# Second gate of a three-layer kernel: half of the rectifier of token chunks 0 and 1 moved to ScalarE, and a new order of its instructions

## The chip, the cores and the metric

The kernel runs on one core of a Trainium2 chip. The metric is the device time of one execution in microseconds (us). TensorE (PE in the profile, PEld for its weight loads) multiplies, VectorE (DVE), ScalarE (ACT) and GpSimd (POOL) do the elementwise work, and the queue of SyncE (SP) issues nearly all transfers. Each engine works through its own instructions strictly in order.

## What is computed

Attention in the Nystroem form gives 2304 rows of 512 values. Two gated layers follow; the change lies in the second one and in the order of everything around it.

```python
def _moe_ref(x, w_in, w_out):
    h = x @ w_in
    return ((h * np.cos(h)) @ w_out)

def _moe2_ref(x, w_in, w_out, alpha):      # x: 2304x512, w_in: 512x2048, w_out: 2048x512
    h = x @ w_in
    g = np.maximum(h, 0.0) + alpha * np.minimum(h, 0.0)
    return (g @ w_out)
```

`alpha` has one value for each of the 2048 columns of `h`. In the kernel `h` lies transposed, so that `alpha` is one value for each partition.

## The kernel before

Every matmul operand is split into a rounded high part and the remainder, and a product is the sum of three matmuls (high by high, high by low, low by high). A split costs a copy to the rounded type on ScalarE and a subtraction (`sub`, line 414) on VectorE or GpSimd.

The first gate runs in 128 ticks, t0 to t127 in the order table (lines 1063 to 1088). The second gate takes the 2304 tokens in four chunks of 512 and one of 256. Each chunk has eight ticks; a tick makes 256 of the 2048 hidden columns, as 128 and 128. Ticks b0 to b7 are chunk 0, b8 to b15 chunk 1, and so on to b39. This text calls them by these names.

In chunks 0 and 1 a tick is `btick`. Its `h` comes from seven Strassen products of six matmuls each (`strassen`, line 1425 in the trace), written into two banks of PSUM that appear as `h` and `x`. Four short copies take partial sums out of these banks (`keep`; line 409 when on ScalarE, 411 when on VectorE): two of them go to the buffer `sa`, two to `sb`, and there is one of each buffer. Some products write again the quarter of a bank that a copy has just emptied, so they wait for that copy. Two additions on VectorE (`cross`, line 1448) then put the tick's 128x1024 result together in the buffer `H`: the first frees bank `x` and `sb`, the second bank `h` and `sa`.

Then each half of the tick (128x512) goes through the rectifier: on VectorE, line 1721 makes alpha\*min(h,0) and line 1724 adds max(h,0). Line 1726 rounds the result on ScalarE, line 414 makes the remainder, and twelve matmuls of 512 columns (line 1738) multiply it by `w_out` and add into four banks `acc`.

Chunks 2 and 3 use `mtick` with `narrow` (products in line 1469, copies through line 409 or 411, additions in line 1481) and a Strassen form of the second product too (line 1620). Their rectifier has a first half on ScalarE: line 1555 makes max(h,0), line 1557 makes max(-h,0) in place, and line 1559 on VectorE multiplies the latter by -alpha (`minus`) and adds. Chunk 4 has a direct product (line 1524) and its rectifier on VectorE alone.

Weights of the second gate are made once, spilled to DRAM (`wf2d`) and loaded again for each chunk from chunk 1 on, into buffers that are used again as soon as the last product has read them (line 1267 issues these loads; `y_load`, `load_wo2` and `t_make` load the rest).

The order is written out: `ORDER` is a table of some 4,200 names, and `Plan.go` emits the operations in that order, each on the engine that its suffix names. So the table decides what stands before what on every engine, and which of two engines does a copy or a subtraction. Buffers and waits follow from the data.

Of the kernel before, what the change touches and what calls it, by code (L numbers as in the profile page):

```python
# [142 lines left out]
t120:7/V y0:29 y0:18 t118:9 t119:9 t123:1 t122:2 o1:2 t121:7/V t122:3 t118:10 t118:8 t120:9 t119:8 t119:10 t120:8 y0:9
t122:4 t123:2 y0:34 y0:15/V y0:10/V t122:5 s64:10 t123:3 t123:4 t123:5 y0:39 t122:6 t124:1 y0:35/V o9:2 y0:30 t122:7
t123:6 t123:7 o1:3 t120:10 t121:10 t121:9 t125:1 t122:9 t123:9 t120:11 t121:8 t121:11 y0:19 t124:2 t124:3 t124:4 t124:5
t127:1 t122:8 t125:2 y0:27 t125:3 y0:28/V t125:4 y0:20 s65:3 o9:3 t125:5 y0:40/V t127:2 t127:3 t124:6 t127:4 t122:10
t123:10 t126:1 t122:11 t123:8 t123:11 t124:7/V t125:6 t126:2 o10:1 o11:1 s65:1 s64:25 c62:5 o0:1 t124:8 t127:5 t127:6
t125:7 t127:7/V t126:3 t126:4 t126:5 t126:6 t126:7/V o10:2 b0:1 b0:2 b0:4 t124:9 b0:3/V b0:5 b0:6/V b0:7 b0:8 b0:9 b0:10
b0:13 b0:11 b0:12 b0:14 o11:2 o11:3/V o10:3 t125:8 b1:1 o4:1 s65:4 s64:7 t124:10 b1:2 b1:4 b1:5 o0:2 b1:3 o4:2 s65:8
t126:8 o8:1 b0:15 o0:3/V o6:1 t125:9 t124:11 t126:9 s65:5 s65:11 s65:9/V s65:6/V b1:6/V s65:14/V s65:18/V s65:22/V  # L150
s65:15 s65:16/V s65:12/V s65:26/V t125:11 t126:11 t127:11 t125:10 t126:10 b1:7 b1:8 t127:10 b1:9 b1:10 b2:1 t127:8 o8:2
b0:16 o6:2 s65:10 o4:3/V s65:27 e127:5/V b0:22 b2:2 s65:28/V b2:4 s65:17 s66:3 b1:13 s65:23 s65:24 s65:19 b2:3 b1:11/V
b1:12 s65:20 b2:5 t127:9 s65:13 s65:25 b2:7 b2:6 b2:8 b2:9 b2:10 b3:1 b3:2 o8:3/V b0:23 b0:17 e127:2 s65:7 b1:14 b2:13
e127:1 e127:4 b0:24 b0:25 b0:20 b1:15 b1:22 b1:16 b2:11 b0:21 b0:18 b3:4 s66:4 s66:2 b1:23 b1:17/G o6:3 b2:12 b3:5
b3:3/V b3:7 s66:11 b3:6 b1:24 e127:6 s65:29 s66:8 s66:1 b0:19 e127:3 s66:12/V b2:22 b3:8 s66:5 b3:9 s66:6 s66:13 b1:25/G
s66:9/V s66:14/V s66:15 s66:16/V b2:23 b2:14 s66:18/V s66:22 o3:1 s66:17 s66:10 s65:21 o2:1 b0:26 b1:18 s66:26/V o3:2
s66:27 s66:23 s66:24 b2:15 s66:28/V s66:7 o12:1 b3:10 b4:1 b3:13 b3:11/V b2:24 s66:19 s66:20 s67:2 s66:25 b0:27 b0:28
b4:2 b0:29 b2:16 b4:3/V b4:4 b4:5 o2:2 b2:25/G b1:19 b1:27 b1:21 b1:20 b1:28 s67:1 b3:12 b2:17/G s66:29 b4:7 b4:6 b1:26
s67:3 b4:8/V b1:29 b4:9 b4:10 b5:1 b5:2 b5:4 s67:4 b4:13 o2:3/V b2:19 b2:27 b5:5 b3:14 b3:15 o3:3/V s67:8 b3:16 b3:17/G
o14:1 s66:21 b4:11/V b5:3/V b2:18 b2:20 b2:21 b2:28 s67:5 b4:12 b3:22 b2:26 b3:18 b5:6/V b3:20 s67:11 s67:12/V b3:23  # L160
b4:22 b3:24 s67:6/V b4:23 s67:9/V s67:14/V b3:25 b4:14 b5:7 s67:15 b5:8 b5:9 s67:18 s67:22 o13:1 o13:2 o13:3/V s67:26/V
b2:29 b3:21 b3:19 s67:23 o12:2 b5:10 b6:1 b6:2 b3:29 b4:15 o12:3/V s67:24/V b5:11 b4:16 s67:16/V o14:2 b5:12 b5:13 o14:3
# [10 lines left out]
b10:3/V b10:6/V b7:19 b9:15 b10:7 b10:9 b10:8 b7:27 b10:10 b10:11 b8:24 b8:25 b11:1 b11:2 b11:4 x7:2 b7:37 s69:2 b9:16
b10:12 b9:17 b9:22 b9:23 b10:13 b10:14 b11:5 b9:24 b9:25 b7:29 b8:21 b8:19 b8:27 b7:30 b11:3/V x7:3/V b8:18 b11:6/V
b10:15 x7:4/V b11:7 b8:20 b11:8/V b11:9 b11:10 x7:11 b10:16 s69:7 s69:4 x7:5 x7:6 b8:28 b9:20 b8:29 b9:19 x7:9 x7:7
b11:11 b7:28 s69:1 x7:12/V b10:22 b10:23 b11:12 x7:8 s69:3 x6:2 b10:17 b9:21 b9:29 x6:1 b8:26 s69:5 b10:24 b10:25 b11:13
x6:3 x6:4 x7:10 b9:18 b9:26 b11:22 b11:23 s69:6 x6:11 x6:12 b7:31 b11:14 b11:15 x5:1 b11:16 b11:24 b12:1 b12:2 b12:3/V
x6:5 x5:2 b11:25 b11:17 b12:4 b12:5 b9:28 b12:7 b12:6 b12:8 b12:9 b10:20 b12:10 b13:1 b13:2 b13:4 s70:1 b12:11 x6:7
b12:13 x5:3/V x6:6/V x6:9 b12:12 b10:18 b9:27 x6:10/V b12:14 x6:8 y2:2 s70:2 x4:1 x4:2 b10:19 b13:5 x5:4/V b13:3 s70:3
b10:28 x5:5 x5:6 b10:21 b10:29 b13:7 s70:4 b12:15 b12:16 x5:7 b13:6 b13:9 b12:22 b12:17 b13:8/V b12:23 b10:27 b11:20  # L180
b13:10 b10:26 b11:21 b11:18 b11:26 b14:1 b12:24 s70:7 x5:8 x5:9 x5:11 x4:3 x4:4 x4:5 x4:6 x5:12 x4:7 x4:9 b11:19 b14:2
b13:11 b13:12 b13:13 s70:6 x3:2 b14:3/V b13:22 b12:25 x4:10/V b13:23 b14:4 b11:27 x5:10 x4:8 b14:5 y2:1 b14:6 s70:5
# [1626 lines left out]
```

## Time and profile before

| | |
|---|---|
| median of three runs | 798.35 us (797.6 to 801.91) |
| profiled execution, its own time | 795.35 us |
| its span, first to last instruction | 793.5 us |
| TensorE busy in the span | 776.8 us, 98% |
| VectorE, ScalarE, GpSimd busy | 640.2, 437.6, 240.0 us |
| TensorE clock granted | 1.000 of full speed over the span |

The profile is one execution. Its span leaves 1.85 us of its own time to what lies around it. A busy TensorE is read with care: the ends of matmuls are modelled, so that short waits can lie inside the busy time, and the weight loads (PEld) are shown apart. A wait is put down to what ended it.

The stages of the second half stand in the trace like this: the second gate's first product (tick b0) starts at 403.6 us, chunks 0 and 1 run to about 566 us, chunks 2 and 3 to about 746 us, chunk 4 to 789 us; then the last stores land.

### The profile page before, as it was taken

Reading aid. Unit: us, or ns where it says so; the run is one execution under the profiler, and the core shown is the slowest. Engines: PE = TensorE matmul, PEld = TensorE weight load, DVE = VectorE, ACT = ScalarE, POOL = GpSimd, SP = SyncE. Lnnn points to the kernel's source line nnn. Section 1 sums busy time; section 2 is a strip of 40 time slices with the busy share of each in tenths; the row PEclk is TensorE's granted clock in tenths of the full one; section 3 lists DMA queues with packets and bytes.
Section 4 is the critical chain, followed back from the end, with each engine's and each line's share of the span. In section 5 each row is a group of like instructions: output and inputs, shape, how many; then the busy total and the mean of one; then the engine's idle time right before and its main releaser. Section 6 shows DMA issues by size and latency. Waiting matters only on the chain. (4 is left out here: it accounts for less than half of the span.)

```text
span 793.5 us, 18121 instructions
## 1 busy us (share of the span) xinstructions
PE 776.8 (98%) x6906; PEld 714.2 (90%) x6906; DVE 640.2 (81%) x1374; ACT 437.6 (55%) x992; POOL 240.0 (30%) x257
## 2 busy tenths in 40 slices
PE   8989999999999999999999999999999999999997
PEld 6577899998988999999998898889889999999997
DVE  4999988788988879888669797676977689776886
ACT  5487666778765555666755343233455475555431
POOL 0334232777323222343534342145311011000200
PEclk9999999999999999999999999999999999999999
DMA  9993447998877657774567854767166514563450
GB/s 284 246 301 129 123 148 170 195 213 175 267 238 250 221 161 261 243 246 135 202 202 269 290 172 158 239 238 266 43 202 227 208 68 139 181 207 125 136 197 28
DMA packets 114278, 154.80 MB, mean 195 GB/s; under 512 B 55568, under 2 KB 73488, under 8 KB 114192
## 3 DMA queue, kind: packets, MB, share of 16 engines
q1 hardware_dynamic: 114032, 153.39, 62.8%
q8 instruction: 54, 0.88, 0.5%
q14 instruction: 32, 0.26, 0.1%
q10 hardware_dynamic: 160, 0.26, 0.1%
HBM read 114.57 MB, written 39.06 MB: 194 GB/s over the span
## 5 line engine op out<-in xcount | busy, mean ns | idle before, releaser
L414 POOL TENSOR_TENSOR m<-m,m 128x288 fp32r<-128x288 f32 (+4 forms) x176 | 176.2, 1014 | 441.3 <-ACT m L1075 138.5
L1088 PE MATMUL acc<-m,m 128*128 128x288 f32 x1536 | 230.9, 298 | 0.0
L1088 PEld LDWEIGHTS acc<-m,m 128*128 128x128 f32 x1536 | 210.6, 188 | 15.3 <-issue 11.9
L414 DVE TENSOR_TENSOR m<-m,m 128x512 fp32r<-128x512 f32 (+5 forms) x268 | 151.9, 587 | 26.5 <-ACT m L1573 12.3
L1063 PE MATMUL h<-m,m 128*128 128x288 f32 x768 | 124.2, 299 | 1.2 <-DVE m L1073 0.7
L1063 PEld LDWEIGHTS h<-m,m 128*128 128x128 f32 x768 | 107.6, 188 | 6.6 <-DVE m L1073 3.8
L1738 PE MATMUL acc<-m,m 128*128 128x512 f32 x384 | 97.3, 394 | 0.0
L1072 ACT ACTIVATE m<-m,quarter 128x288 f32<-128x288 f32 x128 | 67.8, 535 | 44.1 <-DVE m L1070 43.2
L1469 PE MATMUL x<-m,m 128*128 128x256 f32 x588 | 85.6, 286 | 1.8 <-DVE m L414 0.8
L1469 PEld LDWEIGHTS x<-m,m 128*128 128x128 f32 x588 | 75.4, 189 | 4.7 <-ACT m L409 1.4
L1738 PEld LDWEIGHTS acc<-m,m 128*128 128x128 f32 x384 | 68.6, 188 | 11.9
L1073 DVE TENSOR_TENSOR m<-m,h 128x288 f32<-128x288 f32 x128 | 57.0, 449 | 25.6 <-ACT m L1072 20.4
L1573 ACT ACTIVATE m<-m 128x256 fp32r<-128x256 f32 (+2 forms) x96 | 45.8, 508 | 54.1 <-DVE m L1587 21.7
L1068 ACT ACTIVATE m<-h 128x288 int32<-128x288 f32 x128 | 51.5, 404 | 34.5 <-PE h L1063 32.7
L1070 DVE SCALAR_TENSOR_TENSOR m<-h,m 128x288 f32<-128x288 f32 x128 | 57.5, 450 | 15.6 <-ACT m L1068 14.6
L1075 ACT ACTIVATE m<-m 128x288 fp32r<-128x288 f32 x128 | 55.3, 439 | 26.4 <-DVE m L1073 19.8
L1620 PE MATMUL acc<-m,m 128*128 128x256 f32 x485 | 69.0, 281 | 0.1
L1620 PEld LDWEIGHTS acc<-m,m 128*128 128x128 f32 x485 | 62.3, 189 | 0.5 <-ACT m L1573 0.3
L409 ACT ACTIVATE m<-x 128x256 f32<-128x256 f32 (+5 forms) x75 | 29.3, 398 | 38.4 <-PE x L1469 28.6
L574 DVE SCALAR_TENSOR_TENSOR m<-m,m 128x512 int32<-128x512 int32 x64 | 46.7, 734 | 0.3
L572 DVE SCALAR_TENSOR_TENSOR m<-m,m 128x512 int32<-128x512 int32 x64 | 45.3, 711 | 0.3
L1425 PE MATMUL h<-m,m 128*128 128x256 f32 x300 | 43.0, 283 | 0.8 <-ACT m L409 0.8
(176 smaller groups left out, 1121.7 us busy)
## 6 DMA issues: line engine op xcount, KB each, us to landing
m<-wf2d SPq DMA_DIRECT2D x72, 512.0 KB, 4.7
m<-in_moe_w_in_dram SPq DMA_DIRECT2D x32, 512.0 KB, 5.3
m<-in_moe_w_out_dram SPq DMA_DIRECT2D x32, 512.0 KB, 5.5
wf2d<-m SPq DMA_DIRECT2D x28, 512.0 KB, 4.7
m<-w1d SPq DMA_DIRECT2D x32, 256.0 KB, 5.2
m<-wo2d SPq DMA_DIRECT2D x32, 256.0 KB, 3.3
y1d<-m SPq DMA_DIRECT2D x24, 288.0 KB, 4.7
m<-wi2d SPq DMA_DIRECT2D x20, 256.0 KB, 3.8
```

The costliest lines, as they stand in the source:

```text
L414: ENG[e].tensor_tensor(o, a, b, op=ALU.subtract)
L574: op(dve(512), lambda e: nc.vector.scalar_tensor_tensor(cf.t, rv(0), 29, cf.t, op0=ALU.logical_shift_right, op1=ALU.bitwise_or), r=[raw], ...
L1063: nc.tensor.matmul(out=hp.t[:, 0:CW], lhsT=w_[:, js], rhs=x[:, cs], start=(i == 0), stop=(i == 5))
L1068: op(act(CW, True), lambda e: nc.scalar.activation(k_.t, hp.t[:, 0:CW], AF.Copy, scale=INV2PI, bias=0.25), r=[hp], w=[k_], target=T + 0.8)
L1070: op(dve(CW), lambda e: nc.vector.scalar_tensor_tensor(u.t, hp.t[:, 0:CW], INV2PI, k_.t, op0=ALU.mult, op1=ALU.subtract), r=[hp, k_], w=[u])
L1072: op(act(CW), lambda e: nc.scalar.activation(u.t, u.t, AF.Sin, scale=2.0 * math.pi, bias=quarter), rw=[u], aset="sin")
L1073: op(dve(CW), lambda e: nc.vector.tensor_tensor(hc.t, u.t, hp.t[:, 0:CW], op=ALU.mult), r=[hp, u], w=[hc], target=T + 2.6)
L1075: op(act(CW), lambda e: nc.scalar.activation(gh.t, hc.t, AF.Copy), r=[hc], w=[gh, gl])
L1088: nc.tensor.matmul(out=yg[o].t[:, 0:CW], lhsT=w_.t[:, sl], rhs=x.t, start=(j == ja and i == 0), stop=(j == jb and i == 2),)
L1469: nc.tensor.matmul(out=rv(r), lhsT=a_.t[:, p, c2, js], rhs=b_.t[:, q_, c2], start=(first and c2 == 0 and y == 0), stop=(c2 == 1 and y == 2 ...
L1620: nc.tensor.matmul(out=yb.t[:, 256 * (p + yh):256 * (p + yh) + 256], lhsT=a_, rhs=b_, start=(st and p + yh + y == 0), stop=(en and y == 2) ...
L1738: nc.tensor.matmul(out=ya[n][t].t, lhsT=gv(x_), rhs=r_.t, start=(st and k == 0), stop=(en and k == 2))
```

## The change

There are three parts.

1. In `btick`, the rectifier takes the form that `mtick` has: two activations on ScalarE (the second in place in `H`) and one instruction on VectorE, in place of two on VectorE. That is 32 halves.
2. In `strassen`, the two results H03 and H12 become two marks of which each half reads its own. Both additions still write both, so a half still waits for both; the mark lets the in-place activation of one half go without the other.
3. The order table is new from the middle of the first gate's last ticks (t117 to t119) to the end, some 1,900 names. All before is the same.

```diff
@@ the order table, one line of many
-y0:31 t116:6 t119:2 t117:4 y0:23 s64:24/V t119:3 t116:7/V y0:17 s64:29 t119:4 y0:11 t117:5 t118:1 y0:12 y0:6/V t119:5
...
@@ strassen
-        H03, H12 = g.buf(None), g.buf(None)
+        Hx = {x: g.buf(None) for x in (0, 2)}
...
-        op(dve(2 * hw), lambda e: cross(e, Y, sb_, H.t[:, 1:3, 0:hw]), r=[reg[2], reg[3], sb_], w=[H12], hold=[Y, H])
-        op(dve(2 * hw), lambda e: cross(e, X, sa, H.t[:, 0:4:3, 0:hw]), r=[reg[0], reg[1], sa], w=[H03], hold=[X, H])
-        return {x: (H, [H03, H12]) for x in (0, 2)}
+        op(dve(2 * hw), lambda e: cross(e, Y, sb_, H.t[:, 1:3, 0:hw]), r=[reg[2], reg[3], sb_], w=[*Hx.values()], hold=[Y, H])
+        op(dve(2 * hw), lambda e: cross(e, X, sa, H.t[:, 0:4:3, 0:hw]), r=[reg[0], reg[1], sa], w=[*Hx.values()], hold=[X, H])
+        return {x: (H, [Hx[x]]) for x in (0, 2)}
@@ btick
-            op(("DVE", w / 1920.0 + 0.13), lambda e, j=j, m_=m_, hv=hv: nc.vector.tensor_scalar(
-                m_.t[:, 0:w], hv(), 0.0, alpha_sb[:, j:j + 1], op0=ALU.min, op1=ALU.mult),
-                r=[*hr, alb], w=[m_], hold=hold)
-            op(dve(w), lambda e, m_=m_, hv=hv: nc.vector.scalar_tensor_tensor(
-                m_.t[:, 0:w], hv(), 0.0, m_.t[:, 0:w], op0=ALU.max, op1=ALU.add), r=hr, rw=[m_], hold=hold)
+            op(act(w), lambda e, m_=m_, hv=hv: nc.scalar.activation(m_.t[:, 0:w], hv(), AF.Relu), r=hr, w=[m_], hold=hold)
+            op(act(w), lambda e, hv=hv: nc.scalar.activation(hv(), hv(), AF.Relu, scale=-1.0), rw=hr, hold=hold)
+            op(dve(w), lambda e, j=j, m_=m_, hv=hv: nc.vector.scalar_tensor_tensor(
+                m_.t[:, 0:w], hv(), minus[:, j:j + 1], m_.t[:, 0:w], op0=ALU.mult, op1=ALU.add), r=[*hr, alb], rw=[m_],
+                hold=hold)
```

Over the whole program TensorE has the same matmuls as before. VectorE has 38 instructions fewer: 32 of the rectifier go, 17 subtractions move to GpSimd, and 11 copies come from ScalarE. ScalarE has 53 more (64 of the rectifier, less those 11), GpSimd 17 more. The same transfers are issued, in another order. The changed kernel has one line more, so that its line numbers stand one higher.

Two places show how instructions moved. In the rows a name that begins with m\_ is a memory region, not a variable: m\_659 holds `sa`, `sb` and one of the two slots of `H`, m\_577 the other slot, m\_274 and m\_346 hold rectified halves.

The first place is the end of tick b1 and the start of b2. On TensorE, before, from the last product of b1 (first row) to the product of b2 that needs the buffer `sa` (last row):

```order
L1425 MATMUL h<-m_5194,m_5055 128x256 x6
L1425 MATMUL h<-m_4542 128x256 x6
L1088 MATMUL acc<-m_727,m_1131 128x288 x3
L1425 MATMUL h<-m_5160,m_4542 128x256 x6
L1425 MATMUL x<-m_5356,m_4542 128x256 x6
L1425 MATMUL x<-m_5160,m_4867 128x256 x6
L1088 MATMUL acc<-m_727,m_1131 128x288 x3
L1425 MATMUL h<-m_5194,m_5055 128x256 x6
```

The same stretch of TensorE after:

```order
L1426 MATMUL h<-m_5194,m_5055 128x256 x6
L1089 MATMUL acc<-m_727,m_1131 128x288 x3
L1089 MATMUL acc<-m_727,m_1722 128x288 x3
L1089 MATMUL acc<-m_727,m_1131 128x288 x3
L1089 MATMUL acc<-m_727,m_1722 128x288 x3
L1089 MATMUL acc<-m_727,m_1131 128x288 x3
L1426 MATMUL h<-m_4542 128x256 x6
L1089 MATMUL acc<-m_727,m_1131 128x288 x3
L1426 MATMUL h<-m_5160,m_4542 128x256 x6
L1426 MATMUL x<-m_5368,m_4542 128x256 x6
L1426 MATMUL x<-m_5160,m_4867 128x256 x6
L1426 MATMUL h<-m_5194,m_5055 128x256 x6
```

Between the same two products stand two groups of the first gate's matmuls before, and six after.

On VectorE at that place, before (the third row is the addition that frees `sa`):

```order
L1721 TENSOR_SCALAR m_346<-m_577,alpha_sb 128x512
L414 TENSOR_TENSOR m_5055<-m_154,m_5055 128x512
L1448 TENSOR_TENSOR m_659<-h,m_659 128x2x256
L411 COPY m_659<-h 128x256
L1448 TENSOR_TENSOR m_659<-x,m_659 128x512
```

and after:

```order
L1724 SCALAR_TENSOR_TENSOR m_274<-m_577,minus,m_274 128x512
L1246 TENSOR_TENSOR m_154<-m_263,m_154 128x512
L1449 TENSOR_TENSOR m_659<-h,m_659 128x2x256
L1246 TENSOR_TENSOR m_230<-m_230,m_154 128x512
L412 COPY m_659<-h 128x256
L415 TENSOR_TENSOR m_1132<-m_1178,m_1132 128x512
L1449 TENSOR_TENSOR m_659<-x,m_659 128x512
```

The subtraction that stood just ahead of the addition has gone behind it.

The second place is ScalarE in tick b8. Before, with the tick's copy out of bank `h` in the last row:

```order
L1318 ACTIVATE m_5194<-m_1330 128x256
L554 ACTIVATE m_1131<-m_1178 128x512
L1318 ACTIVATE m_5356<-m_154 128x256
L1318 ACTIVATE m_5356<-m_1374 128x256
L1318 ACTIVATE m_5194<-m_1374 128x256
L409 ACTIVATE m_659<-h 128x256
```

and after:

```order
L1319 ACTIVATE m_5368<-m_1328 128x256
L410 ACTIVATE m_659<-h 128x256
L1722 ACTIVATE m_346<-m_577 128x512
L1319 ACTIVATE m_5194<-m_1328 128x256
L1723 ACTIVATE m_577<-m_577 128x512
L410 ACTIVATE m_659<-h 128x256
```

After, both activations of a rectifier and one split stand between two of the tick's copies.

## Rows read from the trace of the kernel before

**Rows 1.** Busy time by stretch: time, PE, PEld, DVE, ACT, POOL, clock, DMA, GB/s.
```profile
404.00:566.00 162.00, 160.44 (x1037) 145.64 (x1036) 124.69 (x218) 64.69 (x145) 58.58 (x54) 1.00 0.65 223
566.00:746.00 180.00, 178.20 (x1416) 172.88 (x1415) 140.36 (x282) 98.43 (x203) 19.84 (x22) 1.00 0.47 162
746.00:789.50 43.50, 42.66 (x354) 41.85 (x352) 36.91 (x112) 13.14 (x36) 2.82 (x2) 1.00 0.34 109
```

**Rows 2.** Weight loads' waits after 378 us: who, for whom, us, times, longest.
```profile
PEld x L1469 <- DVE m L1481: 1.8, 5, 0.7
PEld x L1469 <- ACT m L409: 1.4, 5, 0.4
PEld x L1425 <- ACT m L409: 1.2, 2, 0.9
PEld h L1425 <- ACT m L409: 1.1, 1, 1.1
PEld x L1469 <- DVE m L414: 0.9, 1, 0.9
PEld h L1620 <- DVE m L414: 0.6, 1, 0.6
PEld h L1425 <- DVE m L411: 0.4, 1, 0.4
PEld acc L1620 <- ACT m L1573: 0.3, 1, 0.3
PEld x L1469 <- DMA m<-wf2d: 0.2, 1, 0.2
PEld h L1425 <- ACT m L1726: 0.2, 1, 0.2
PEld acc L1620 <- DVE m L414: 0.2, 1, 0.2
```

**Rows 3.** Groups by line: instruction, count | busy us, mean ns | idle before.
```profile
L1738 PE MATMUL acc<-m,m 128*128 128x512 f32 x384 | 97.3, 394 | 0.0
L1721 DVE TENSOR_SCALAR m<-m,alpha_sb 128x512 f32<-128x512 f32 x32 | 17.6, 551 | 2.0 <-POOL m L414 1.7
L1724 DVE SCALAR_TENSOR_TENSOR m<-m,m 128x512 f32<-128x512 f32 x32 | 24.1, 759 | 0.3
L1559 DVE SCALAR_TENSOR_TENSOR m<-m,minus,m 128x512 f32<-128x512 f32 x32 | 24.6, 788 | 3.3 <-ACT m L1557 3.1
L1555 ACT ACTIVATE m<-m 128x512 f32<-128x512 f32 x32 | 20.0, 626 | 18.5 <-DVE m L1481 12.1 <-DVE m L1587 3.4 <-DVE m L414 2.8
L1557 ACT ACTIVATE m<-m 128x512 f32<-128x512 f32 x32 | 19.9, 629 | 0.7
L409 ACT ACTIVATE m<-h 128x256 f32<-128x256 f32 (+3 forms) x37 | 14.9, 407 | 32.3 <-PE h L1425 24.9 <-DVE m L1448 5.3 <-PE h L698 2.0
```

**Rows 4.** Timeline around 422 us: start, us, engine, instruction, [idle before].
```profile
420.27 3.06 POOL L414 TENSOR_TENSOR m<-m,m 128x512 fp32r<-128x512 f32 x2 [12.65 <-DMA wf2d<-m]
420.42 1.78 DVE L414 TENSOR_TENSOR m<-m,m 128x512 fp32r<-128x512 f32 x1
420.55 1.55 PE L1425 MATMUL x<-m,m 128*128 128x256 f32 x12
...
422.12 0.68 DVE L1448 TENSOR_TENSOR m<-h,m 128x512 f32<-128x512 f32 x1
422.91 0.38 ACT L409 ACTIVATE m<-h 128x256 f32<-128x256 f32 x1 [2.20 <-DVE m L1448]
...
423.35 0.86 PE L1425 MATMUL h<-m,m 128*128 128x256 f32 x5 [0.84 <-ACT m L409]
```

**Rows 5.** Timeline around 530 us, tick b12.
```profile
530.13 0.95 PE L1425 MATMUL x<-m,m 128*128 128x256 f32 x6 [0.73 <-DMA m<-wf2d]
```

**Rows 6.** Timeline of ScalarE in tick b8.
```profile
487.78 0.38 ACT L409 ACTIVATE m<-h 128x256 f32<-128x256 f32 x1 [4.03 <-PE h L1425]
```

**Rows 7.** Transfers by kind: bytes and median us from issue to landing.
```profile
m<-wf2d SPq DMA_DIRECT2D x72, 512.0 KB, 4.7
```

More of the change, by code (lines that the diff above doesn't have):

```diff
@@ L143 @@
[L143 to L162, printed above, removed]
@@ L173 @@
[L173 to L182, printed above, removed]
@@ L243 @@
[L243 to L247 removed]
+y0:31 t116:6 t119:2 t117:4 y0:23 s64:24/V t119:3 t116:7/V y0:17 s64:29 t117:5 y0:11 t119:4 t117:6 t117:7 y0:6 e111:3
@@ new lines @@
+t118:1 o1:1 t118:2 t118:3 t118:4 t119:5 y0:12/V t118:5 t118:6 t118:7/V t116:9 t117:9 t116:8 t115:11 t120:1 t120:2 t121:1
+t121:2 s64:7 t117:8 t119:6 y0:24 t120:3 y0:13 y0:18/V t120:4 y0:14 t118:9 t116:10 t117:10 t116:11 t117:11 t118:11
+t118:10 t119:7/V t121:3 t120:5 y0:32/V t121:4 t119:11 t122:1 t120:6 t121:5 o1:2 o1:3/V t118:8 y0:9 t122:2 t120:7 y0:25
+y0:26 t122:3 y0:33/V y0:37 y0:15 t121:6 t119:9 t122:4 t122:5 t123:1 t121:7 s65:2 o9:1 t119:8 t123:2 t123:3 t123:4 t120:8
+y0:38 y0:27 y0:29 t122:6 t122:7/V t123:5 y0:10/V t119:10 t120:10 t120:9 s64:25 t124:1 y0:39 t123:6 t124:2 t121:9 t120:11
@@ new lines @@
+b10:11 b9:16 b9:17 b9:18/G b9:26 b11:6/V b11:7 b8:19 b10:12 b7:30 b8:20 b8:31 x7:1 b8:21 x7:2 b11:8/V b9:27 b8:30 b11:9
+x7:3/V x6:1 x7:4 x6:2 b10:14 b10:23 b10:24 b10:25 x6:3 b10:26 b10:15 b8:29 b9:21 x7:11 s69:2 s69:1 b9:20 b9:30 b10:27
+b9:22 s69:7 b11:10 b9:31 b8:28 x7:12 x6:4/V x6:5 x6:7 x7:7 x7:5 x7:6/V b11:13 x6:8 x7:8 b10:16 s69:4 s69:3 s69:6 x5:2
+b12:1 b12:2 s69:5 x7:9 b11:11 x7:10 x6:6 b10:17 b10:18 x5:1 b12:3/V b11:12 b12:4 b9:19 b12:5 b12:7 b12:6/V b12:9 b12:8/V
+b12:10 b13:1 b13:2 b9:29 x6:11 b10:20 b11:23 b11:24 b11:14 b11:15 b11:16 b11:25 x5:3 b12:11/V b12:13 b13:3/V x5:4 x5:5
@@ new lines @@
+b11:17 b11:26 b11:27/G x6:12/V b12:12 b13:4 b9:28 b13:5 b13:7 b13:8 b10:22 s70:3 b10:21 x5:6 b10:30 b12:14 x6:9 x6:10/V
+b11:18 b13:6 b13:9 b12:15 x5:9 x5:7 b12:16 b10:19 b13:10 b10:28 x5:8/V s70:1 x4:2 s70:2 b14:1 x4:1 x5:10 x4:3 x4:4
+b12:17 b13:11/V b12:18 b13:12 s70:5 x5:11 s70:7 b12:23 b12:24 b10:29 b11:21 b11:30 b10:31 b11:22 b13:13 x5:12 x4:7
+b13:14 b11:20 s70:4 b14:2 x4:5/V x4:6/V s70:6 x4:9 b13:15 b13:16 b14:3 x4:10 x3:2 x3:1 x4:8/V b12:25 b11:19 x4:11 b14:4
+b14:5 b14:6 x3:3/V b14:7 b14:8 b12:26 b14:9 b14:10 x4:12 b11:29 b15:1 b15:2 b14:11 y2:2 y2:21 y2:22 b13:17 x3:4 b12:27/G
@@ new lines @@
+b11:31 y2:3 x3:7 y2:4 y2:16 x3:8 x3:5 y2:17 b12:22 b15:4 b15:5 b14:13 b13:18 b13:23 y2:36 b15:6 y2:23 b13:24 b15:3/V
+b14:12 x3:6/V x3:9 b14:23 y2:5/V y2:37/V b11:28 b15:7 b15:8/V b15:9 b15:10 y2:6 y2:24/V b13:25 y2:9 b14:24 b12:20 b12:21
+b12:19 b13:26 y2:7 b15:11 b13:27/G y2:25/V b15:13 y2:26/V b16:1 b16:2 y2:29 b14:14 y2:31 y2:11 b15:12 b12:28 b12:29
+b12:30 b14:25 b13:20 y2:12/V y2:32/V b14:26 x3:10 y2:13/V b12:31 b13:19 b13:28 b13:21 b13:22 x0:2 y2:18/V y2:10/V b14:27
+x3:11 b16:3 b14:15 b14:16 y2:19 y2:14 y2:15/V x3:12 x0:1 y2:33 y2:34 y2:27 b15:23 y2:35 b16:4 b16:5 b14:17 b14:18 b13:31
```

167 lines of the change are left out of this document (89 added, 78 removed).

## The prediction

> **What bounds the kernel now.** Begin with the busy time by stretch [rows 1]. Only the second half matters, since the order is the same up to t117. TensorE is busy for 160.44 of 162 us in chunks 0 and 1, 178.20 of 180 us in chunks 2 and 3, 42.66 of 43.5 us in chunk 4. It is the bound in all three stretches, and the change gives it the same matmuls. Its idle time adds up to 1.56 + 1.80 + 0.84 = 4.20 us. VectorE is at 124.69 of 162 us (77%) in chunks 0 and 1, ScalarE at 64.69 (40%).
>
> Then read the waits of the weight loads [rows 2], which start ahead of their matmuls and so show a wait that the modelled end of a matmul hides. They add up to 8.3 us. Line 1425 belongs to chunks 0 and 1: 1.2 + 1.1 + 0.4 + 0.2 = 2.9 us. Lines 1469 and 1620 belong to the later chunks: 5.4 us. So what a better order can give is between 4.2 and 8.3 us, 0.5% to 1.0% of the profiled 795.35 us, and that only if no wait at all is left. Faster VectorE work gives nothing by itself; it counts only where TensorE waits for it.
>
> A measurement of this kernel can tell about 0.5%, 4 us, from no change. That is nearly all of the idle time of TensorE.
>
> The Trainium skill, Perfetto Trace Analysis, section Identifying the Most-Contended Engine, says that matmul busy time misjudges the distance from the limit and that the busy share of LDWEIGHTS should be used. Here that share is 145.64 of 162 us in chunks 0 and 1 [rows 1], which would leave 16.4 us, and a better order might then give 10 us or more. This trace speaks against it: the 384 matmuls of 512 columns take 394 ns each and are preceded by no idle time [rows 3]; there the loads wait for the matmuls, and only 2.9 us of the 16.4 us are waits for other engines [rows 2]. I give that outcome 0.02, inside the chance of faster.
>
> **The change part by part.**
>
> *The rectifier's work.* VectorE loses 32 instructions of line 1721 (17.6 us) and 32 of line 1724 (24.1 us) and gets 32 like line 1559 (24.6 us): 17.1 us less. ScalarE gets 64 like lines 1555 and 1557, 20.0 + 19.9 = 39.9 us [rows 3]. In chunks 0 and 1 that takes VectorE from 77% to about 66% and ScalarE from 40% to about 65%. Neither becomes the bound. One half's way from addition to split is 551 + 759 ns before and 626 + 629 + 788 ns after, 0.73 us longer. Cover: a half's second product comes some ticks after its first, with ten microseconds or more of other matmuls between by the order rows, so this is hidden and costs 0. If the cover were gone, it would be 0.73 us for each of the halves that lost it.
>
> *The wait at 422 us.* At 420.27 us GpSimd starts a subtraction; the one that VectorE starts at 420.42 us takes 1.78 us [rows 4]. Behind it stands the addition that frees `sa` (422.12 us), for that the copy on ScalarE waits (422.91 us, 2.20 us idle), and for the copy the product at 423.35 us, 0.84 us of idle TensorE; its load waited 1.1 us [rows 2, 4]. After the change that subtraction stands behind the addition, and six groups of three first-gate matmuls stand between the two products where there were two. Three matmuls of 288 columns take some 0.4 us (an estimate by columns from the twelve of 256 in 1.55 us, tail included [rows 4]), so the copy has 1.6 us more. The wait goes: between -0.84 and -1.1 us; I take -1.0. What is late next there is nothing that the rows show.
>
> *The wait at 530 us.* A product of tick b12 waits 0.73 us for a load of `wf2d`, and its weights 0.9 us behind a copy [rows 2, 5]. The loads go into buffers as the last reader leaves them. Going by the order and 0.7 us for six matmuls (twelve take 1.55 us with the tail of the last [rows 4]), a load has at least some 5.6 us of products between the last use and the next in the new order, 6.3 us in the old, against a median landing of 4.7 us [rows 7]. So this wait can go (-0.9) or come back at another load (+0.5 net, if two such loads are late). I take -0.8, near to the row, since the loads of this weight group are issued in another order and none stands at the smallest room there.
>
> *The copies of the ticks in chunks 0 and 1.* What stands behind the new activations on ScalarE is the tick's copies, and for these TensorE waits. The new order has 33 of the 64 copies on ScalarE (35 before). Where a product that frees a quarter is followed by one product only and then by the one that needs the quarter, the room is 0.7 us, and a copy takes 0.41 us [rows 3]. Counted from the order there are 6 such places before and 14 after, of 32. At the six, one waited (the one at 530 us, for the transfer), so a place without anything ahead of its copy costs nothing. In tick b8, though, ScalarE now has an activation, a split of 256 columns and another activation between two copies. From the start of the first copy to the end of the second that is 0.41 + 0.63 + 0.41 + 0.63 + 0.41 = 2.5 us, while TensorE has three products, 2.1 us, from there to the product that needs the second copy. Before, the second copy found ScalarE idle for 4.03 us [rows 6]. Price: 0 to 0.7 us; I take +0.5. For the other seven new places I take +0.3 in all, between 0 (the copy finds its engine free) and 7 x 0.63 = 4.4 us (each stands behind a whole activation).
>
> *The 28 other changes of engine.* VectorE: 17 subtractions fewer, 11 copies more. They change loads by some microseconds over 400 us, off the path: 0.
>
> *Chunks 2 to 4.* The work is the same, only the order differs. Of the 5.4 us of waits, 1.8 us are for the additions of line 1481 and 1.4 us for copies [rows 2]. The product of the tick that follows such an addition has the same room in the new order in nearly all 16 ticks of chunks 2 and 3, so these come back. The bounds are -2.6 us (1.80 + 0.84, all idle time gone) and as much the other way; I take 0. The last eight products of chunk 4 have much the same work of VectorE ahead of them.
>
> Sum: -1.0 - 0.8 + 0.5 + 0.3 + 0 = -1.0 us, from 795.35 to 794.35 us for the profiled execution. That execution was 3.0 us below the median of the three runs; applied to the median, 798.35 - 1.0 = 797.35, so 797.3 us.
>
> **The rivals.**
>
> *Faster.* VectorE was the engine whose lateness let TensorE wait, and the 17.1 us taken from it let the search remove most waits. Then all idle time goes in chunks 0 and 1 (1.56 to 2.9 us) and half of that of the rest (1.3 to 2.7 us), with some 0.1 us of restart for each of about a dozen waits: -4 to -6.5 us, 792 to 794 us. For it: the chain at 422 us starts on VectorE, and 0.9 + 1.8 + 0.6 us of the other waits name it [rows 2]. Against it: three of the four rows of line 1425 name ScalarE, which gets the work.
>
> *Slower: activations that wait at the head of ScalarE.* Before, the rectifier began on VectorE, behind the addition that it reads, in the same queue. Now it begins on ScalarE with a wait for VectorE, and all copies behind it wait too, as the copy at 422.91 us did for 2.20 us [rows 4]. TensorE then stands for what exceeds 0.7 to 2 us of room. If 8 of the 32 halves cost 0.7 us, that is +5.6 us, less 1.8 us of waits removed: +3.8, 802.2 us; if 12, +6.6, 805 us. It decides from about 8 halves on. For it: ScalarE at 65%, 14 places with the least room. Against it: the same form runs in chunks 2 and 3, where ScalarE is at 98.43 of 180 us and its copies cost 1.4 us in all [rows 1, 2].
>
> The Trainium skill, ScalarE: Activation LUTs, section Rules for kernel authors, says the opposite of the change: relu, max and add belong on VectorE, not on ScalarE. By it the change is a loss. The rows agree on the price (1.31 us of VectorE become 2.04 us on two engines [rows 3]); whether time is lost depends on the copies behind.
>
> *No effect: the waits only change places.* Then the time is 798.35 us. It can't be told from my forecast.
>
> **How the numbers follow.** The forecast with its neighbours, no effect among them, has 0.62: 794.5 to 802 us. Faster has 0.20, slower (over 802.3 us) 0.18. For 8 in 10 the range takes in half of the faster rival and the milder form of the slower one, 793.0 to 802.5 us. Faster by over 0.5% means below 794.4 us.
>
> **What would show it.** Right: line 1425's waits fall from 2.9 to below 2 us, the wait in tick b2 is gone, one of about 0.5 us behind line 410 stands in tick b8, those of line 1469 (1470 after) stay at 3 to 6 us, VectorE in chunks 0 and 1 is at some 65%, ScalarE at some 63%. Wrong: copies on ScalarE ended by waits of the first activation for line 1449, or a new wait of over 1 us for a transfer, or waits in chunks 2 to 4 that differ from 5.4 us by more than 3.

## The result: slower by 0.7%, against a forecast of no change

| | before | after |
|---|---|---|
| median | 797.37 us (20 runs, 794.56 to 801.91) | 802.64 us (20 runs, 798.5 to 806.96) |
| ratio after/before | | 1.0068, 95% interval 1.0056 to 1.0081 |
| profiled execution, its span | 793.5 us | 800.8 us |

The forecast was 797.3 us, range 793.0 to 802.5. The change costs 4.5 to 6.5 us (the interval times 797.37), and its time lies outside the range by a hair and on the side that had a chance of 0.18.

The two programs are the same up to t117, and yet the second gate's first product starts at 403.6 us in the profile of before and at 407.2 us in that of after. In the twelve profiles of this study it starts between 403.5 and 407.9 us, and kernels of both orders lie at both ends. So the profiles are compared from there on. The stages below run from the first product of one stage to the first of the next, and the last to the end of the last matmul; they are worked out from the matmuls of each trace.

| | chunks 0 to 3 | chunk 4 | both |
|---|---|---|---|
| before | 334.4 us | 51.25 | 385.6 |
| before, profiled a second time (below) | 333.05 | 51.25 | 384.3 |
| after | 333.9 | 55.34 | 389.2 |

All of the loss that these rows show is in chunk 4: 4.1 us.

The busy time of after by stretch, the same view as [rows 1]; the columns are length, PE, PEld, DVE, ACT and POOL busy (with counts), clock, DMA share, GB/s:

```profile
404.00:566.00 162.00, 160.81 (x1050) 146.00 (x1048) 114.33 (x183) 97.39 (x201) 70.62 (x63) 1.00 0.65 225
566.00:746.00 180.00, 179.45 (x1410) 173.67 (x1409) 143.23 (x281) 99.89 (x206) 30.19 (x32) 1.00 0.48 164
746.00:789.50 43.50, 39.74 (x321) 39.33 (x320) 33.98 (x96) 11.48 (x31) 4.13 (x3) 0.96 0.33 110
```

TensorE's idle time went from 1.56 to 1.19 us in chunks 0 and 1, from 1.80 to 0.55 us in chunks 2 and 3, and from 0.84 to 3.76 us in the last stretch, which also shows a clock of 0.96. The waits of the weight loads, the view of [rows 2], say who is waited for:

```profile
PEld x L1525 <- DVE m L1552: 4.2, 2, 2.8
PEld h L1426 <- ACT m L410: 1.6, 3, 0.7
PEld x L1470 <- DVE m L1482: 1.3, 4, 0.4
PEld x L1426 <- DVE m L412: 0.8, 2, 0.6
PEld x L1470 <- ACT m L410: 0.6, 3, 0.2
PEld x L1426 <- ACT m L410: 0.5, 2, 0.3
...
PEld x L1470 <- DMA m<-wf2d: 0.4, 1, 0.4
PEld x L1470 <- issue: 0.3, 1, 0.3
PEld h L1426 <- issue: 0.3, 1, 0.3
PEld acc L1621 <- DVE m L415: 0.2, 1, 0.2
```

The first row is new. Line 1525 is the direct product of chunk 4, line 1552 the second rectifier instruction there. No such row stood in [rows 2]. The timeline of TensorE and VectorE at the longer of the two waits (start, us, engine, instruction, count, idle before):

```profile
750.38 1.60 PE L1525 MATMUL x<-m,m 128*128 128x256 f32 x12
...
752.08 1.23 DVE L1588 TENSOR_TENSOR m<-m 128x128 f32<-128x128 f32 x1
...
753.41 0.48 DVE L1549 TENSOR_SCALAR m<-x,alpha_sb 128x256 f32<-128x256 f32 x1
753.82 0.41 DVE L1643 TENSOR_TENSOR m<-h,m 128x256 f32<-128x256 f32 x1
754.15 0.41 DVE L1552 SCALAR_TENSOR_TENSOR m<-x,m 128x256 f32<-128x256 f32 x1
...
754.62 3.67 PE L1525 MATMUL x<-m,m 128*128 128x256 f32 x18 [2.64 <-DVE m L1552]
...
757.05 0.48 DVE L1549 TENSOR_SCALAR m<-x,alpha_sb 128x256 f32<-128x256 f32 x1 [2.15 <-PE x L1525]
```

In chunk 4 a tick computes its two halves with twelve matmuls each, into the two halves of one bank `x`: b33:1 and b33:2 in the order table. b33:3 and b33:4 are the rectifier of the first half (lines 1549 and 1552 here), b33:5 and b33:6 that of the second. The row at 750.38 is b33:1, the one at 754.62 begins with b33:2. b33:2 writes another half of the bank than the one that b33:4 reads; it needs nothing that VectorE makes. It waits for b33:4 all the same. The new table shows why. Before, b33:2 follows b33:1 at once, and b33:3 comes later; after, b33:3 and b33:4 are issued ahead of b33:2:

```text
before: b33:1 b33:2 b32:14 b32:20 b34:1
after:  b33:3 b31:49 b33:4 b31:54 s80:2 s79:3 b33:2 b34:1
```

The kernel's own plan gives the two halves marks of their own, but the waits of the built program go by the bank: what is issued later waits for the earlier user of the same bank. In the trace the first matmul of b33:2 carries a wait for VectorE in after, and none in the kernel below that issues it early. On TensorE nothing moved; b33:2 stands right behind b33:1 there, before and after. The Trainium skill, PSUM — Partial Sum Buffer, section PSUM bank collisions raise a hardware error, says that two engines must not touch one bank in the same partitions at once, even at disjoint columns, and that PSUM is to be guarded by the bank, not by the address. This trace agrees with a guard by the bank: the 2.64 us end with the reader of the other half. That an unguarded product would fail was not tried.

Then the clock. Rows of the same columns as above, the wait and what follows it:

```profile
751.70:754.60 2.90, 0.27 (x3) 0.07 (x1) 2.79 (x7) 1.15 (x5) 1.26 (x1) 1.00 0.61 136
754.60:758.20 3.60, 3.58 (x19) 3.58 (x20) 1.41 (x4) 0.42 (x2) 0.00 (x0) 0.60 0.39 123
```

After 2.64 us without a matmul the granted clock is 0.60 on the mean of the next 3.6 us, that is 1.2 GHz for most of them and 2.4 GHz for the rest. The 18 matmuls at 754.62 us take 3.67 us, 204 ns each.

The second new wait is tick b38, of the same form (b38:3 and b38:4 stand ahead of b38:2 in the new table):

```profile
783.05 0.42 DVE L1552 SCALAR_TENSOR_TENSOR m<-x,m 128x256 f32<-128x256 f32 x1
...
783.52 0.97 PE L1525 MATMUL x<-m,m 128*128 128x256 f32 x6 [1.12 <-DVE m L1552]
```

### The profile page after: what moved, and what is told of

Read it like the earlier page. It is cut to its first block, busy times and chain, and to the rows that moved or that the text cites. A ratio compares the mean times of both kernels' runs of the same rounds, so it can differ in the third digit from the quotient of the medians.

```text
span 800.8 us, 18151 instructions
## 1 busy us (share of the span) xinstructions
PE 781.2 (98%) x6906; PEld 716.4 (89%) x6906; DVE 633.3 (79%) x1336; ACT 470.2 (59%) x1045; POOL 260.8 (33%) x274
## 4 chain that ended last, share of the span: by engine, by line
PE 74%; DMA 9%; DVE 9%; ACT 4%; issue 2%; SPq 1%; POOL 0%; DVEq 0%; ACTq 0%
PE acc L1089 19%; PE x L1470 10%; PE acc L1739 10%; PE h L1064 10%; PE acc L1621 7%; PE h L1426 5%; PE x L1426 4%; PE x L1525 3%; PE h L1621 3%; DMA m<-in_moe_w_in_dram 3%; DMA m<-in_moe_w_out_dram 2%; PE x L1020 1%; DVE m L415 1%; PE x L1621 1%; PE x L957 1%
## 5 line engine op out<-in xcount | busy, mean ns | idle before, releaser
L415 POOL TENSOR_TENSOR m<-m,m 128x288 fp32r<-128x288 f32 (+4 forms) x194 | 196.3, 1025 | 442.0 <-ACT m L1076 156.0
L415 DVE TENSOR_TENSOR m<-m,m 128x512 fp32r<-128x512 f32 (+4 forms) x250 | 149.3, 617 | 20.5 <-ACT m L1574 6.6
L1574 ACT ACTIVATE m<-m 128x512 fp32r<-128x512 f32 (+2 forms) x96 | 45.6, 508 | 53.0 <-DVE m L1552 20.1
L410 ACT ACTIVATE m<-x 128x256 f32<-128x256 f32 (+5 forms) x69 | 27.0, 400 | 35.2 <-PE x L1470 25.0
```

Of the source, the lines that this page charges most:

```text
L415: ENG[e].tensor_tensor(o, a, b, op=ALU.subtract)
```

## The experiments

Three theories of the 5 us were tested first. A: the two products wait for a reader of their bank because of where they are issued, and the clock falls behind the first wait. B: VectorE simply has too much to do ahead of chunk 4's rectifier in the new order. C: the activations on ScalarE cost the time, in chunks 0 and 1. The times of all kernels stand here; each ratio is to the kernel before on the same chip, and the stages are those of the table above.

| kernel | median us | ratio, 95% interval | chunks 0 to 3 | chunk 4 |
|---|---|---|---|---|
| after | 802.64 | 1.0068, 1.0056 to 1.0081 | 333.9 | 55.34 |
| after_two_early | 798.15 | 1.0020, 1.0000 to 1.0040 | 334.1 | 51.02 |
| after_b33_early | 797.86 | 1.0020, 1.0004 to 1.0036 | 333.4 | 51.44 |
| after_b38_early | 803.44 | 1.0088, 1.0065 to 1.0111 | 334.75 | 54.82 |
| before_b33_late | 801.38 | 1.0060, 1.0041 to 1.0079 | 334.3 | 55.26 |
| before_again | 796.50 | 0.9996, 0.9979 to 1.0013 | 333.05 | 51.25 |
| after_fill | 799.16 | 1.0035, 1.0019 to 1.0051 | 333.7 | 53.82 |
| after_early_no_part1 | 801.06 | 1.0048, 1.0019 to 1.0078 | 337.6 | 51.01 |
| before_part1_alone | 809.21 | 1.0162, 1.0136 to 1.0188 | 345.0 | 51.25 |
| after_early_tidied | 796.56 | 0.9994, 0.9977 to 1.0012 | 332.0 | 50.64 |
| after_early_no_gpsimd | 801.07 | 1.0054, 1.0035 to 1.0073 | 337.7 | 51.00 |

### Both products issued early

```diff
@@ after, the order table, tick b33
-b33:3 b31:49 b33:4 b31:54 s80:2 s79:3 b33:2 b34:1
+b33:2 b33:3 b31:49 b33:4 b31:54 s80:2 s79:3 b34:1
@@ tick b38
-b36:23 b38:3 b36:15 b36:16 b38:4 b37:17 s83:3 b38:2 b36:21
+b36:23 s83:3 b38:2 b38:3 b36:15 b36:16 b38:4 b37:17 b36:21
```

> The changed kernel with two names moved in the table: the second product of tick b33 is issued ahead of the rectifier of the first half of b33 (with it nothing else moves), and the second product of b38 (with the subtraction of its weights) ahead of the rectifier of the first half of b38. Every engine has the same instructions in the same order; only what waits for what changes, since both halves of such a tick lie in one bank of PSUM. Theory A (the two products wait for a rectifier that they don't need, and the clock falls to half behind the first wait): the waits of 2.64 and 1.12 us at line 1525 go, the clock stays at 1.00 near 755 us, and some 2.6 + 1.7 + 1.1 = 5.4 us go: 797 to 798.5 us against 802.6 us. Theory B (VectorE has too much ahead of chunk 4's rectifier in the new order): the products go at once, but a later product waits for the same late rectifier; 800 to 802 us. Theory C (the activations on ScalarE cost it in chunks 0 and 1): 802 to 803 us.

No engine's order changes by this edit: in the second gate the two traces show the same instructions in the same order on every engine. Only what waits for what changes. The timeline at the same place, of this kernel:

```profile
749.65 3.75 PE L1525 MATMUL x<-m,m 128*128 128x256 f32 x30
...
751.35 1.26 DVE L1588 TENSOR_TENSOR m<-m 128x128 f32<-128x128 f32 x1
...
752.72 0.48 DVE L1549 TENSOR_SCALAR m<-x,alpha_sb 128x256 f32<-128x256 f32 x1
...
753.23 0.88 PE L1525 MATMUL x<-m 128*128 128x256 f32 x6
```

TensorE goes through 30 matmuls and on without a gap. VectorE is as late as in after: the rectifier of b33 starts 3.07 us after the start of b33:1 here (752.72 - 749.65) and 3.03 us in after (753.41 - 750.38). So its lateness by itself costs nothing, and theory B falls. The ratio to before drops from 1.0068 to 1.0020, chunk 4 by 4.3 us. The median, 798.15 us, is what theory A gave (797 to 798.5); theory C gave 802 to 803. The 0.2% that is left is taken up below.

### Each of the two alone

> The changed kernel with the second product of b33 alone issued ahead of the rectifier of b33's first half. Theory A: the wait of 2.64 us and the slow clock behind it go, the one of 1.12 us at b38 stays: about 4.3 us less, 798 to 799 us. Theory B: 800 to 802 us. Theory C: 802 to 803 us.

> The changed kernel with the second product of b38 alone (and its weights' subtraction on GpSimd) issued ahead of the rectifier of b38's first half. Theory A: the wait of 1.12 us goes, that of b33 and the slow clock stay: about 1 us less, 801 to 802 us. Theories B and C: 802 to 803 us.

b33 alone gives 3.9 of the 4.3 us in chunk 4 (55.34 to 51.44) and the same median as both. b38 alone gives 0.5 us there (55.34 to 54.82); its median, expected at 801 to 802 us, came out at 803.44, with an interval that holds the ratio of after. The 1.12 us of wait were not worth 1.12 us, because another wait stands behind them: with b38:2 early, a product at 780.09 us of after_two_early waits 0.68 us for a remainder on VectorE (line 415).

### The kernel before with b33:2 issued late

```diff
@@ before, the order table, tick b33
-b33:1 b33:2 b32:14 b32:20 b34:1 b32:15 b32:7 b31:44 b31:50 b32:8 s79:2 s79:3 s80:1 s80:2 b34:2 b31:45 b33:3 b33:5 b33:4 b33:7
+b33:1 b32:14 b32:15 b32:7 b31:44 b31:50 b32:8 b31:45 b33:3 b33:4 b33:2 b32:20 b34:1 s79:2 s79:3 s80:1 s80:2 b34:2 b33:5 b33:7
```

> The kernel before with the second product of b33 issued behind the rectifier of b33's first half, as the changed kernel has it. Each engine keeps its order, but for two rectifier instructions of b33 that change places on VectorE. Theory A: the product starts only when line 1551 of b33's first half has ended, at some 751.8 us in place of 749.35: a wait of 2.4 us, then the clock at half for some 3.4 us (1.7 us more): about 4 us slower than before, 801 to 802 us. Theories B and C: this is not what costs the time, below 1 us slower.

The loss can be put into the kernel before by this alone: 0.6%, chunk 4 from 51.25 to 55.26 us. The wait in its timeline and the busy time behind it:

```profile
753.61 0.42 DVE L1551 SCALAR_TENSOR_TENSOR m<-x,m 128x256 f32<-128x256 f32 x1
...
754.08 2.85 PE L1524 MATMUL x<-m,m 128*128 128x256 f32 x12 [2.21 <-DVE m L1551]
```

```profile
754.10:757.50 3.40, 3.40 (x16) 3.40 (x17) 0.53 (x2) 0.31 (x1) 0.00 (x0) 0.51 0.13 51
```

A wait of 2.21 us, and the clock at 0.51. This kernel has none of the change's activations and, outside tick b33, none of its order.

### What the clock costs by itself

```diff
@@ after, the direct product of chunk 4 (n is the chunk, i the tick in it, x the half)
-                    for k, (a_, b_) in enumerate(ab):
+                    for k, (a_, b_) in list(enumerate(ab)) * (2 if n == 4 and i == 1 and x == 0 else 1):
```

> The changed kernel with the first product of b33 computed twice (the second time over the same place, with the same result), so that TensorE works for 1.43 us of the 2.64 us in which it waits. The wait for the rectifier is not touched. If the slow clock comes from the idle time ahead of it: the wait reads about 1.2 us, the clock stays at 1.00, and the 1.7 us of matmuls at half the clock go: 801 us against 802.6. If the slow clock comes from the place in the program or from what VectorE and GpSimd do there: the clock falls as before, 802.6 us.

The twelve matmuls of b33:1 run twice in the time in which TensorE waited:

```profile
747.60 3.02 PE L1525 MATMUL x<-m,m 128*128 128x256 f32 x24
751.86 2.41 PE L1525 MATMUL x<-m,m 128*128 128x256 f32 x18 [1.24 <-DVE m L1552]
```

```profile
751.86:755.40 3.54, 3.54 (x29) 3.54 (x30) 2.01 (x7) 0.71 (x2) 0.00 (x0) 1.00 0.60 199
```

b33:2 starts 4.26 us after b33:1, as in after (4.24 us), but the clock stays at 1.00, and the 18 matmuls take 2.41 us, not 3.67. Chunk 4 is shorter by 1.5 us (55.34 to 53.82). So of the 3.9 us of b33 some 2.4 are the wait and 1.5 the clock behind it. The median fell to 799.16 us, further than the 801 us expected; as a ratio, 801 us is 1.0046, inside the interval (1.0019 to 1.0051). The mean granted clock of each run says the same: one fall takes some 0.002 off it (0.40 of 3.6 us in 800.8, from the row of after), and it is 0.999 or 1.000 in all 12 runs here, 0.995 to 0.999 in the 20 of after. Work that only kept TensorE busy made the kernel faster, which is the plainest sign that idle time ahead of the slow stretch is its cause.

### How far two sets of runs lie apart

> The kernel before, unchanged, timed as if it were another. It tells how far two sets of runs of one program lie apart: the ratio should hold 1.000 within 0.2%. If it does not, the 0.2% by which the changed kernel with its two products issued early is above the kernel before is no more than the scatter.

0.9996, interval 0.9979 to 1.0013. From the first product of the second gate to the end it took 384.3 us against 385.6 of the first profile; 0.7 us of that is the wait for a transfer at 530 us, which the second profile lacks. The ratio held 1.000 within 0.2%, so the scatter between two sets does not by itself account for the 0.2% of after_two_early. That 0.2% isn't shown either: its interval begins at 1.0000, that of after_b33_early at 1.0004, and the profile of after_two_early (385.1 us from the first product on) lies between the two of before.

### The rectifier back on VectorE, in the new order

```diff
@@ after_two_early, btick
-            op(act(w), lambda e, m_=m_, hv=hv: nc.scalar.activation(m_.t[:, 0:w], hv(), AF.Relu), r=hr, w=[m_], hold=hold)
-            op(act(w), lambda e, hv=hv: nc.scalar.activation(hv(), hv(), AF.Relu, scale=-1.0), rw=hr, hold=hold)
...
+            op(("DVE", w / 1920.0 + 0.13), lambda e, j=j, m_=m_, hv=hv: nc.vector.tensor_scalar(
+                m_.t[:, 0:w], hv(), 0.0, alpha_sb[:, j:j + 1], op0=ALU.min, op1=ALU.mult),
+                r=[*hr, alb], w=[m_], hold=hold)
...
```

> The changed kernel with its two products issued early, and the rectifier of chunks 0 and 1 back on VectorE alone, as two instructions in the places of the first activation and of the last instruction. The order is else the same. If the activations on ScalarE gain (VectorE was what TensorE waited for): waits in chunks 0 and 1 grow and it is 2 to 4 us slower than with them. If they cost (they stand ahead of TensorE's copies): it is 1 to 3 us faster. If they are neutral: within 1 us from b0 to the end, VectorE back from 71% to some 80% of chunks 0 and 1.

```profile
404.00:566.00 162.00, 158.33 (x1033) 143.84 (x1032) 127.72 (x208) 64.07 (x140) 70.06 (x61) 1.00 0.65 225
```

VectorE is at 127.72 us, 79%, and TensorE's idle time in chunks 0 and 1 is 3.67 us, against 1.72 us with the activations. Chunks 0 to 3 take 337.6 us, 3.5 more than with them. The waits that are new or longer than in after_two_early name VectorE first: 1.40 us for a copy on it (line 411) in tick b4, and 1.43 us in the first ticks of chunk 2 for an addition on it (line 1481); a wait for a copy on ScalarE in b7 grew from 0.25 to 0.77 us. In this order, then, the activations on ScalarE gain 3.5 us by the profiles, and theory C falls. The medians give less (1.0048 against 1.0020, 0.3%), with intervals that overlap; that the activations cost nothing is sure, the size of the gain is not.

### The activations alone, in the old order

The code of the change with the table of before; each pair of activations takes the place of the instruction of line 1721, and the names behind it in a tick are counted up. In tick b0, for example:

```diff
@@ before, the order table with the code of after
-b0:10 b0:13 b0:11 b0:12 b0:14 o11:2
+b0:10 b0:13 b0:11 b0:12 b0:14 b0:15 o11:2
```

> The kernel before with the two activations on ScalarE in the place of the first rectifier instruction of chunks 0 and 1, in the order of before. By the rival of the prediction (an activation that waits at the head of ScalarE's queue holds TensorE's copies): 4 to 6.6 us slower, since this order was not made for it. By the prediction's own sum (0.7 us for each copy held, few places): 0 to 3 us slower.

It is slower by 1.6%, 12 us, more than any theory gave. Its waits of weight loads, and the longest of them in the timeline:

```profile
PEld h L1426 <- DVE m L412: 6.2, 4, 2.7
PEld x L1470 <- issue: 2.7, 2, 2.5
PEld h L1426 <- ACT m L410: 2.2, 4, 0.7
```

```profile
524.11 0.63 ACT L1722 ACTIVATE m<-m 128x512 f32<-128x512 f32 x1 [1.42 <-DVE m L1449]
...
525.30 0.61 ACT L1727 ACTIVATE m<-m 128x512 fp32r<-128x512 f32 x1
...
526.00 0.69 DVE L415 TENSOR_TENSOR m<-m,m 128x512 fp32r<-128x512 f32 x1 [1.93 <-ACT m L1727]
526.61 0.42 DVE L412 COPY m<-h 128x256 f32<-128x256 f32 x1
...
527.08 0.98 PE L1426 MATMUL h<-m,m 128*128 128x256 f32 x6 [2.31 <-DVE m L412]
```

VectorE stands at a remainder (line 415) for 1.93 us, since the rounding that it reads (line 1727) now comes behind two activations on ScalarE; the tick's copy stands behind that remainder on VectorE, and TensorE waits 2.31 us for the copy. The first of the two activations had itself stood at the head of ScalarE for 1.42 us, for an addition on VectorE (line 1449). So the rival of the prediction is a real mechanism, but most of it comes through the other queue: what ScalarE holds is a rounding, VectorE waits at its head for that, and the copies behind it on VectorE are held. Of TensorE's idle time behind b0, 4.9 us end with copies on VectorE, 2.1 us with an addition on VectorE at the start of chunk 2 and 1.3 us with copies on ScalarE. In the new order the wait of 2.31 us, at tick b11, is not there.

### Small moves beyond the change

```diff
@@ after_two_early, the order table
-s66:8 b1:26 s66:5 b1:27 b3:3 b2:11 b2:12
+b3:3 b2:11 s66:8 b1:26 s66:5 b1:27 b2:12
@@
-o12:3/V b5:16 b6:13
+o12:3/V b6:13 b5:16
@@
-b36:23 s83:3 b38:2 b38:3 b36:15 b36:16 b38:4
+b36:23 b36:15 b36:16 s83:3 b38:2 b38:3 b38:4
```

> The changed kernel with its two products issued early, and three waits of TensorE that are left in its trace taken on by small moves in the table: two copies of tick b3 and b2 ahead of three activations on ScalarE (the product at 435.6 us waits up to 1.3 us for them), the addition b6:13 on VectorE ahead of a rectifier instruction of 1.78 us (the product at 475.7 us waits 0.7 us), and a subtraction of b36 ahead of the rectifier of b38 (a product at 780.1 us waits 0.68 us). If these waits are independent, some 0.3 to 1.3, 0.7 and 0.7 us go, about 2 us: 796 us beside 798.1 for the early version, some 0 to 0.3% below the kernel before. If each only makes room for the next wait: no change, 798 us.

```profile
404.00:566.00 162.00, 161.80 (x1053) 147.49 (x1052) 115.00 (x185) 99.56 (x206) 72.70 (x64) 1.00 0.65 224
566.00:746.00 180.00, 179.62 (x1424) 174.52 (x1424) 143.97 (x283) 97.81 (x201) 28.23 (x31) 1.00 0.48 163
```

TensorE's idle time is 0.20 and 0.38 us in these stretches; the second gate takes 382.6 us, 2.5 less than with the two early products alone and 1.7 and 3.0 less than in the two profiles of before. The median, 796.56 us, is not distinguishable from before (0.9994, 0.9977 to 1.0012). By this view less than 0.6 us of idle time is left in chunks 0 to 3 for moves of instructions to win.

### The remainders back from GpSimd

```diff
@@ after_two_early, the order table, twelve names of this form
-b0:18/G
+b0:18
```

> The changed kernel with its two products issued early, and the 12 remainders of chunks 0 and 1 that its table gives to GpSimd back on VectorE, in the same places. VectorE was forecast at 66% of chunks 0 and 1 and is at 71%: its instructions of 128x512 take longer than before (line 1724 takes 0.88 us against 0.79 forecast, line 415 takes 0.845 against 0.786). If that is GpSimd working beside it, these means fall towards 0.80 and 0.79 us, and VectorE's busy time rises by less than the 12 x 0.7 = 8.3 us that it takes over. If the longer times have another cause, the means stay and it rises by 8 us or more. TensorE from b0 to the end: within 2 us of the early version.

The busiest groups of VectorE between 404 and 566 us (instruction, count, busy us, mean ns, idle before), of after and then of this kernel (after_two_early has means of 846 and 909 ns, like after):

```profile
L415 DVE TENSOR_TENSOR m<-m,m 128x512 fp32r<-128x512 f32 x41 | 34.2, 845 | 6.9 <-ACT m L1727 4.0 <-ACT m L1394 2.3 <-ACT m L555 0.4
L1724 DVE SCALAR_TENSOR_TENSOR m<-m,minus,m 128x512 f32<-128x512 f32 x28 | 24.3, 881 | 7.6 <-ACT m L1723 7.6
```

```profile
L415 DVE TENSOR_TENSOR m<-m,m 128x512 fp32r<-128x512 f32 x51 | 39.7, 789 | 8.6 <-ACT m L1727 5.8 <-ACT m L1394 2.0 <-ACT m L555 0.4
L1724 DVE SCALAR_TENSOR_TENSOR m<-m,minus,m 128x512 f32<-128x512 f32 x28 | 25.3, 914 | 8.2 <-ACT m L1723 8.2
```

VectorE's busy time rises by 3.8 us (113.78 to 117.59), not by 8.3, and line 415 falls to 0.79 us as expected. Line 1724 doesn't: 0.914 us. The reason is seen when the instructions of line 1724 are sorted by whether an instruction of GpSimd runs beside them: in after the 14 without one take 0.745 us, the 14 with one 1.02 us on the mean and up to 1.77; here, 13 and 15, it is 0.745 and 1.06 us. GpSimd's other work (57.75 us in this stretch) still meets this line. The kernel as a whole is 3.6 us slower in chunks 0 to 3, against the 2 us expected at most. Chunks 0 and 1 hardly change (TensorE's idle time is 1.77 us against 1.72). The loss stands at the first ticks of chunk 2, where two products wait 1.50 and 1.04 us for additions on VectorE (line 1482): the work that it took over makes it late there. What GpSimd takes over was worth its price.

## Why the prediction was wrong

**The step that failed** is in the paragraph on chunks 2 to 4: "The last eight products of chunk 4 have much the same work of VectorE ahead of them", with a term of 0 and bounds of 2.6 us either way. The amount of VectorE's work was not the question. What mattered was whether a product of TensorE is issued behind an instruction of VectorE that uses the same bank, and two products were. That is written in the new table (b33:4 ahead of b33:2) and in the waits of the built program, not in either engine's order, and only the orders were compared. The term measures +4.1 us (55.34 against 51.25): some 2.4 us of wait and 1.5 us of clock at b33, and 0.4 to 0.5 us at b38, which add up to the 4.3 us that the two early products give back. The sign of being wrong that was named for chunks 2 to 4 did not show it: their waits add up to 2.8 + 4.2 = 7.0 us, within 3 of 5.4, since it looked at the sum and not at a new row. The upper bound was wrong too, since it was taken from the idle time of before; a new wait, and a clock that falls behind it, is not bounded by the waits that were there.

**Chunks 0 to 3** were forecast at -1.0 us and came out within the scatter: 333.9 us against 334.4 and 333.05. That is in part luck, since misses of either sign stand in it. Term by term:
- VectorE: 17.1 us less forecast, 10.4 us measured (124.69 to 114.33, 71% and not 66%). The activations come to what was forecast (625 ns each; 59 of the 64 lie in the stretch, and ScalarE is at 60%). What was mis-sized first is the duration of VectorE's instructions: line 1724 was put at 0.788 us from [rows 3] and takes 0.881, line 415 of 128x512 takes 0.845 us where it took 0.786. It is beside GpSimd that they are long. Of the 32 instructions of line 1559, from which the price was taken, 5 had GpSimd beside them in before; of the 32 of line 1724 in after it is 16, and without it either form takes 0.745 us. The rows at 420 us [rows 4] had shown this, 1.78 us for one subtraction, and the sum didn't carry it over. The rest is other work in the stretch, such as the 11 copies from ScalarE (5.5 us over the whole program), which the forecast of 66% left out, as it did the 17 subtractions.
- The wait at 422 us: forecast gone; a load still waits 0.7 us for a copy of that tick, where it waited 1.1 (0.3 to 0.6 us in the kernels made from after that keep the activations). Part of it went.
- The wait at 530 us, -0.8: it doesn't appear in the second profile of before either, and in the new order a product of the same tick waits 0.34, 0.58 and 0.98 us for such a load in after_b38_early, after_b33_early and after_fill, and not at all in after. A wait that comes and goes from execution to execution was taken for a property of the order.
- Tick b8, +0.5: no wait there. The other places with the least room, +0.3: the waits of line 1426 add up to 3.2 us, from 2.9 of line 1425 [rows 2]; the sign of being right was below 2. The new ones stand at b3, b5 and b7.
- Chunks 2 and 3: 5.4 us of waits became 2.8, inside the bounds.
- The 17 subtractions to GpSimd, "off the path: 0": not so in this order; with twelve of its remainders back from GpSimd, VectorE is late at chunk 2 and it costs 3.6 us.

**What was right:** TensorE is the bound, and what a better order can give is its idle time. after_early_tidied takes nearly all of that, and the 1.7 to 3.0 us which it gains in the profiles can't be told from no change in the medians (0.9977 to 1.0012). The 4 us that the prediction set for that was too coarse: with 12 runs the interval is some 1.4 us to either side. The outcome by the busy share of LDWEIGHTS, put at 0.02, did not come: that share would still leave 14.5 us there in chunks 0 and 1 (147.49 of 162 us) with TensorE idle for 0.20 us.

**The rivals.** "Activations that wait at the head of ScalarE" had the right sign and nearly the right time (802.2 us), by luck and not by its cause: with the activations and without the two late products all but 0.2% of the loss is gone, and taking the activations out again costs 3.5 us by the profiles. The same mechanism, mostly through VectorE's queue, costs 12 us where the order isn't made for it. The Trainium skill, ScalarE: Activation LUTs, section Rules for kernel authors, says that relu and max belong on VectorE. The runs bear that out in the old order (12 us lost) and not in the new (3.5 us gained). "No effect" is the one that the sum would have come to without chunk 4: with the two products early, chunks 0 to 3 take 334.1 us, as before. "Faster" (its own terms add up to as much as 6.8 us, not 6.5) did not come; even after_early_tidied gains less than its 4 us.

**What stays open.** The medians lie 5.3 us apart, and chunk 4 accounts for 4.1 us of it in the profiles. Where the other 1.2 us lie was not settled; the interval of the change begins at 4.5 us. Nor is it settled what lets the clock fall (below).

## What to carry to other kernels

When an order changes, compare for each matmul what it waits for, not only what stands ahead of it on its engine: where waits go by the PSUM bank, as here, two products into one bank are to be issued together, ahead of the first reader of either. A share of work moved to another engine and the order around it are one change: the same two activations cost 12 us in the old order and gain 3.5 us, by the profiles, in the new. And a bound for a stage that is reordered must leave room for a wait that isn't there yet.
